# Moving buffers, a transpose and a layer norm in a fused routing attention + MLP kernel

## The chip, the cores and the metric

The kernel runs on one core of one Trainium2 chip, in one launch. The metric is the device time of one execution in microseconds (us): the median of some runs. Engines are TensorE (PE: matmuls, PEld: its weight loads), VectorE (DVE), ScalarE (ACT), GpSimd (POOL, hardly used here) and SyncE (SP, whose queue issues nearly all DMAs). Each engine works off its own instructions in order and waits on semaphores for the others.

## The reference

```
# attention: q, k, v (4, 8, 768, 64), 16 centroids a head
q_assign = argmax(normalize(q) . normalize(centroids)); k_assign likewise
mask   = q_assign == k_assign                 # only same cluster
attn   = softmax(where(mask, q k^T / 8, -1e9))
x      = (attn v) as (4, 768, 512)            # heads side by side
# MLP with a layer norm in front, g_ln its weights
xn     = (x - mean(x)) / sqrt(var(x) + 1e-6) * g_ln
out    = x + relu(xn @ w_ch1) @ w_ch2         # 512 -> 2048 -> 512
```

All inputs but the weights of the MLP are 32-bit floats; w_ch1 and w_ch2 come as 64-bit floats and are turned into 32-bit ones on VectorE, bit by bit, in 32 chunks.

## The kernel before

**Attention.** The work goes over 16 pairs of heads (4 sequences times 4 pairs, numbered 0 to 15). A pair has 12 steps: a step makes the scores of 128 keys against 384 queries for both heads (`scores`, L312: four matmuls into `s_ps`, then ScalarE's exp into a tile `e`) and weighs the values with them (`weigh`, L332, into `a_ps`). VectorE adds each `e` into `es`, the sum for the denominator (L350, L353). Two steps are a slot, six slots (0 to 5) a pair; scores run two steps ahead of the weighing. There are five buffers for `e`, so an exp waits until VectorE has added the `e` of five steps before.

Into the slots other work is put, in a fixed order for TensorE, VectorE and ScalarE (a manual schedule): the next pair's transposes (L230) and cluster assignment (`simT_ps`, L263, in slot 2; VectorE's `best`, `hit`, `first` and the two `onehot` tiles, L270 to L282; their transposes, `oh_ps`, L295, in slot 4), the pair before's denominator (`finish`, L363: `den_ps` in slot 1, in slot 3 the reciprocal and the DMAs that spread it as `rb`, in slot 5 the product `x` and its DMA to memory, `xT_d`), two chunks of weights a pair, and by the table `extra` (`put`, L472) what else is due: the sums of weight blocks `ws` (L166, two in each of pairs 8 to 11) and the layer norm of sequence 0.

**Layer norm of a sequence.** `norm_load` fetches x transposed (`xn`), `norm_rows` transposes 128 rows back (`x_ps`, L412), copies them (`xr`), stores them and takes their statistics (`bn`, `mv`); `norm_stats` makes mean and 1/std of all rows (`stat`, with a square root on ScalarE, L426), transposes them (`stat_ps`, L430) and stores them; `norm_row` fetches them as rows over all partitions; `norm_apply` subtracts (L444) and multiplies (L446), four instructions of VectorE each. `x_sum` (L467) then makes the sums `xt` that the first layer needs.

**MLP.** Per sequence, `first_layer` (L595) makes 16 hidden tiles of 128 x 384 for each half of the rows from seven sums of block products (parts 1 to 7; `x_ps`, `y_ps`, `z_ps`), in which VectorE's `add_relu` (L588) and ScalarE's `kept` (L583) take results out of PSUM. `h0` and `h1` are the tiles of the two halves. Then `project` (L636) makes the six output tiles of the second layer (t = 0 to 5; `o_ps`, 32 matmul instructions each), and between them stands the next sequence's layer norm: its load after t = 0, its rows after t = 1 and t = 2, its statistics, rows and application after t = 2. Only TensorE's order is fixed here; the other engines' order is a scheduler's.

**Memory.** Pools of SBUF lie one behind the other in the order in which they are opened. The pools of attention are closed before the MLP's are opened, and these lie on the same memory: `loads` (12 KB a partition), `heads` (18), `route` (3), `attn` (34.5: `e` first, then `es`, `x`, `dsb`, `rb`) and `conv` (12). The MLP's one pool `ffn` (79 KB) covers them all. `x`, `dsb` and `rb` of pair 15 are the last things that attention uses.

Of the kernel before, what the change touches and what calls it, by code (L numbers as in the profile page):

```python
# [8 lines left out]
F32 = mybir.dt.float32  # L9
# [10 lines left out]
def kernel(  # L20
# [11 lines left out]
    nc = tc.nc  # L32
    B, H, S, D = q.shape
    NCL = centroids.shape[1]
    DM, FF = moe_w_ch1.shape
    P = 128
    NT = S // P
    NHALF = 2
    TH = NT // NHALF
    HC = TH * P  # L40
    Q = 32
    NPAIR = H // 2
    NDC = DM // P
    NFC = FF // P
# [6 lines left out]
    xpool = ctx.enter_context(tc.tile_pool(name="xpool", bufs=1))  # L51
# [4 lines left out]
    def pool(name, bufs, **kw):  # L56
        return stage.enter_context(tc.tile_pool(name=name, bufs=bufs, **kw))

    loads = pool("loads", 1)
    heads = pool("heads", 2)  # L60
    route = pool("route", 1)
    attn = pool("attn", 2)
    conv = pool("conv", 1)
    dram = pool("dram", 4, space=bass.MemoryType.DRAM)
    ps_s = pool("ps_s", 2, space=PSUM)
    ps_a = pool("ps_a", 1, space=PSUM)
# [2 lines left out]
    def ps(name, dt=F32, n=512):  # L69
        return pools["t"].tile([P, n], dt, tag="t", name=name)  # L70
# [24 lines left out]
    ident = const.tile([P, P], F32, name="ident")  # L95
# [211 lines left out]
    xs = {}  # L307
# [24 lines left out]
    def weigh(i):  # L332
        n, g, c = steps[i]
        e = soft[i]
        if c == 0:
            accs[n, g] = ps_a.tile([P, 512], F32, tag="a", name="a_ps")
        acc = accs[n, g]
        for j in range(2):
            nc.tensor.matmul(  # L339
                acc[j * D : (j + 1) * D, :HC],  # L340
                loaded[n]["v"][:, c, j, :],
                e[:, j, :],
                start=(c == 0),
                stop=(c == NT - 1),
            )

        if c == 1:
            es = attn.tile([P, 2, HC], F32, tag="es", name="es", bufs=3)
            sums[n, g] = es
            nc.vector.tensor_tensor(es, soft.pop(i - 1), soft.pop(i), ALU.add)  # L350
        elif c > 1:
            es = sums[n, g]
            nc.vector.tensor_tensor(es, es, soft.pop(i), ALU.add)  # L353
        if c == NT - 1:
            if g == 0:
                xs[n] = attn.tile([P, S], F32, tag="x", name="x", bufs=2)
            nc.scalar.copy(xs[n][:, g * HC : (g + 1) * HC], accs.pop((n, g))[:, :HC])


# [3 lines left out]
    def finish(n, part):  # L363
        b, pr = pairs[n]
        if part == 0:
            den = ps("den_ps")
            for j in range(2):
                for g in range(NHALF):
                    r = (j * NHALF + g) * Q
                    nc.tensor.matmul(  # L370
                        den[r : r + Q, :HC], ones, sums[n, g][:, j, :],
                        start=True, stop=True, tile_position=(0, r),
                    )
            dsb = attn.tile([P, HC], F32, tag="dsb", name="dsb", bufs=1)
            nc.scalar.copy(dsb, den[:, :HC])
            for r in range(0, P, Q):
                nc.sync.dma_start(out=rdens[r : r + Q, n, :], in_=dsb[r : r + 1, :])
        elif part == 1:
            nc.vector.reciprocal(rdens[:, n, :], rdens[:, n, :])
            row = dram.tile([2, S], F32, tag="row", name="row")  # L380
            nc.sync.dma_start(
                out=row.rearrange("j (p e) -> (j p) e", e=DE), in_=rdens[:, n, :]
            )
            rb = attn.tile([P, S], F32, tag="rb", name="rb", bufs=1)
            for j in range(2):
                nc.sync.dma_start(
                    out=rb[j * D : (j + 1) * D, :],
                    in_=row[j : j + 1, :].to_broadcast([D, S]),
                )
            late[n] = rb  # L390
        else:
            x = xs.pop(n)
            nc.vector.tensor_tensor(x, x, late.pop(n), ALU.mult)
            nc.sync.dma_start(out=xT_d[b][pr], in_=x)
# [6 lines left out]
    def norm_load(b):  # L401
        xn = xpool.tile([P, NDC, S], F32, tag="xn", name="xn")
        for c in range(NDC):
            nc.sync.dma_start(out=xn[:, c, :], in_=xT_d[b][c])
        mv = small.tile([P, NT, 2], F32, tag="mv", name="mv")
        normed[b] = [xn, mv]
# [15 lines left out]
    def norm_stats(b):  # L422

        _, mv = normed[b]
        stat = small.tile([P, 2, NT], F32, tag="stat", name="stat")
        nc.scalar.activation(stat[:, 1, :], mv[:, :, 1], AF.Sqrt, bias=eps)  # L426
        nc.vector.tensor_copy(stat[:, 0, :], mv[:, :, 0])
        nc.vector.reciprocal(stat[:, 1, :], stat[:, 1, :])
        sp = ps("stat_ps")
        nc.tensor.transpose(sp[: 2 * NT, :P], stat.rearrange("p s t -> p (s t)"), ident)  # L430
        st = small.tile([2 * NT, P], F32, tag="st", name="st")
        nc.scalar.copy(st, sp[: 2 * NT, :P])
        nc.sync.dma_start(out=stat_d[b].rearrange("s (t p) -> (s t) p", p=P), in_=st)

    def norm_row(b, i):
        row = xpool.tile([P, S], F32, tag="row", name="stat_row", bufs=2)
        nc.sync.dma_start(out=row, in_=stat_d[b][i : i + 1, :].to_broadcast([P, S]))
        normed[b].append(row)

    def norm_apply(b, i, c):  # L440
        xn, row = normed[b][0], normed[b][2 + i]
# [30 lines left out]
    def put(n, slot, f, *args):  # L472
        extra.setdefault((n, slot), []).append(lambda: f(*args))

    put(5, 2, norm_load, 0)
    for t in range(NT):
        put(6 + t, 5, norm_rows, 0, t)
    put(12, 2, norm_stats, 0)
    put(12, 2, norm_row, 0, 0)
    for i in range(2):  # L480
        for c in range(NDC):
            put(13 + i, (2, 3, 4, 5)[c], norm_apply, 0, i, c)
    put(12, 3, norm_row, 0, 1)
    for i in range(4):
        for o in range(2):
            put(8 + 2 * o + i // 2, (0, 3)[i % 2], weight_sum, i, slice(o * WC, (o + 1) * WC))
# [78 lines left out]
    ps_m = pool("ps_m", 2, space=PSUM)  # L565
    pools["t"] = pool("ps_o", 3, space=PSUM)
    ffn = pool("ffn", 2)
    hidden = {}

    def product(bank, lhs, rhs, cols, first):  # L570
# [5 lines left out]
            )  # L576

    def hidden_tile(r, f):
        h = ffn.tile([P, HC], F32, tag=f"h{r}", name=f"h{r}", bufs=NFC + 1)
        hidden[r, f] = h  # L580
        return h

# [43 lines left out]
            add_relu(1, j, st["z"], st["u2"])  # L626

    def rows_load(b, t):
        x = ffn.tile([P, DM], F32, tag="xb", name="xb", bufs=3)
        nc.sync.dma_start(out=x, in_=x_d[b][:, t, :])  # L630
        return x

# [3 lines left out]
    def project(b, t, x, fs, op):  # L636
        r, tt = divmod(t, TH)
        for f in fs:
            nc.tensor.matmul(  # L639
                op,  # L640
                hidden[r, f][:, tt * P : (tt + 1) * P],
                w2[:, f, :],
                start=(f == chunks[0]),
                stop=(f == chunks[-1]),
            )
        if fs[-1] != chunks[-1]:
            return
        o = ffn.tile([P, DM], F32, tag="o", name="o_sb")
        nc.vector.tensor_tensor(o, op, x, ALU.add)  # L649
        nc.sync.dma_start(out=out[b].rearrange("(p c) m -> p c m", p=P)[:, t, :], in_=o)  # L650

    with tc.manual_schedule(engines={mybir.EngineType.PE}):
        for i in range(4):
            x_sum(0, i)
        for b in range(B):
            for j in range(NFH):
                for part, ahead in ((1, 0), (2, 0), (4, 1), (6, 0), (3, 1), (5, 0), (7, 0)):
                    if j - ahead >= 0:
                        first_layer(b, j - ahead, part)
            xb = {0: rows_load(b, 0)}  # L660
            for t in range(NT):
                if t + 1 < NT:
                    xb[t + 1] = rows_load(b, t + 1)
                op = ps("o_ps")
                if t == 0:
                    project(b, t, xb[t], chunks[:-2], op)
                    first_layer(b, NFH - 1, 4)
                    first_layer(b, NFH - 1, 3)
                    project(b, t, xb.pop(t), chunks[-2:], op)
                    if b + 1 < B:  # L670
                        norm_load(b + 1)
                else:
                    project(b, t, xb.pop(t), chunks, op)
                if b + 1 < B:
                    if t in (1, 2):
                        for tt in range(TH):
                            norm_rows(b + 1, (t - 1) * TH + tt)
                    if t == 2:
                        norm_stats(b + 1)
                        for i in range(2):  # L680
                            norm_row(b + 1, i)
                            for c in range(NDC):
                                norm_apply(b + 1, i, c)
                        for i in range(4):
                            x_sum(b + 1, i)

    flag = all_in_range()
    stage.close()
# [198 lines left out]
```

## Time and profile before

| | |
|---|---|
| median of 3 runs | 1072.61 us (1071.07 to 1073.33) |
| the profiled execution | 1072.26 us, its span 1070.5 us |
| TensorE busy | 1020.6 us, 95% of the span |
| VectorE, ScalarE busy | 508.3 us (47%), 314.9 us (29%) |
| chain that ended last | PE 88%, DVE 7%, DMA 2%, issue 1%, ACT 1% |
| mean granted TensorE clock | 0.982 of full speed |

The profile describes one execution. Its page gives busy times, the costliest groups of instructions and the chain of work that ended last; the trace can be asked further, as a timeline (start, duration, engine, line, operation, what it writes and reads, and in brackets how long the engine stood idle before and what released it) or as a list of waits. Attention takes about the first 400 us, the four sequences of the MLP the rest.

### The profile page before, as it was taken

What the parts mean: (1) busy time and instruction counts of PE and PEld (TensorE: products, weight loads), DVE (VectorE), ACT (ScalarE), POOL (GpSimd) and SP (SyncE); (2) the same over time, 40 slices, a digit from 0 to 9 for tenths busy, and PEclk for the clock granted to TensorE, in tenths of its full rate; (3) what the DMA queues carried; (4) which work ended last, traced back from release to release, by engine and by line L of the source; (5) the groups of instructions that cost most, each with busy time, mean ns of one, the idle gap of its engine ahead of it and who ended that gap; (6) DMA issues with size and microseconds to landing.
All of it is one profiled execution on the core that took longest, in us unless ns stands there. A gap on an engine that the chain in (4) does not pass through costs nothing.

```text
span 1070.5 us, 11366 instructions
## 1 busy us (share of the span) xinstructions
PE 1020.6 (95%) x4374; PEld 500.8 (47%) x4374; DVE 508.3 (47%) x860; ACT 314.9 (29%) x516; POOL 2.8 (0%) x27
## 2 busy tenths in 40 slices
PE   6999999999989985999999999989999989999997
PEld 3444444444434432554444555434555434555443
DVE  4888888999998983331141221150221150221000
ACT  4566666666666630220100220000221000221000
POOL 1000000000000000000000000000000000000000
PEclk9999999999999997999999999999999999999999
DMA  7344565545454311002221001231000321000100
GB/s 159 99 135 131 146 168 145 138 129 139 125 139 129 99 66 59 1 0 79 77 71 39 1 1 36 93 98 40 0 1 1 127 80 39 20 0 1 40 29 23
DMA packets 104765, 77.62 MB, mean 73 GB/s; under 512 B 84176, under 2 KB 84224, under 8 KB 104704
## 3 DMA queue, kind: packets, MB, share of 16 engines
q1 hardware_dynamic: 104032, 76.79, 24.9%
q8 instruction: 36, 0.59, 0.2%
q14 instruction: 25, 0.20, 0.1%
q10 hardware_dynamic: 672, 0.03, 0.0%
HBM read 57.71 MB, written 19.00 MB: 72 GB/s over the span
## 4 chain that ended last, share of the span: by engine, by line
PE 88%; DVE 7%; DMA 2%; issue 1%; ACT 1%; SPq 0%; DVEq 0%; ACTq 0%
PE o_ps L639 31%; PE x_ps L572 15%; PE a_ps L339 10%; PE s_ps L324 9%; PE z_ps L572 8%; PE y_ps L572 4%; PE s_ps L319 3%; PE qk_ps L230 2%; DVE es L353 2%; PE sim_ps L247 1%; PE oh_ps L295 1%; PE den_ps L370 1%; PE x_ps L412 1%; DMA x_d<-xr 1%; PE simT_ps L263 1%
## 5 line engine op out<-in xcount | busy, mean ns | idle before, releaser
L639 PE MATMUL o_ps<-w,h 128*128 128x512 f32 x768 | 336.8, 599 | 0.0
L639 PEld LDWEIGHTS o_ps<-w,h 128*128 128x128 f32 x768 | 147.3, 192 | 182.2 <-issue 180.1
L329 ACT ACTIVATE e<-s_ps 128x768 f32<-128x768 f32 x192 | 152.0, 812 | 65.5 <-PE s_ps L324 60.4
L324 PE MATMUL s_ps<-t,t 64*128 64x384 f32 x768 | 157.3, 488 | 0.0
L339 PE MATMUL a_ps<-e,v_sb 128*64 128x384 f32 x768 | 144.8, 499 | 0.0
L590 DVE TENSOR_TENSOR h<-z_ps,u 128x384 f32<-128x384 f32 x64 | 35.7, 557 | 208.7 <-PE z_ps L572 131.7
L353 DVE TENSOR_TENSOR es<-es,e 128x768 f32<-128x768 f32 x128 | 122.2, 955 | 9.5 <-ACT e L329 2.8
L649 DVE TENSOR_TENSOR o_sb<-o_ps,xb 128x512 f32<-128x512 f32 x24 | 16.6, 690 | 212.0 <-PE o_ps L639 212.0
L339 PEld LDWEIGHTS a_ps<-e,v_sb 128*64 128x64 f32 x768 | 46.6, 136 | 86.9 <-issue 85.8
L324 PEld LDWEIGHTS s_ps<-t,t 64*128 64x128 f32 x768 | 69.8, 192 | 22.1 <-issue 22.1
L585 ACT COPY u<-x_ps 128x384 f32<-128x384 f32 x64 | 30.6, 478 | 139.7 <-PE x_ps L572 139.7
L585 ACT COPY p<-x_ps 128x384 f32<-128x384 f32 x32 | 15.3, 478 | 167.6 <-PE x_ps L572 154.3
L319 PE MATMUL s_ps<-m,m 64*128 64x384 bf16 x384 | 64.3, 331 | 0.0
L572 PE MATMUL x_ps<-xt,ws 128*128 128x384 f32 x128 | 48.0, 498 | 12.6 <-DMA xb<-x_d 12.6
L572 PE MATMUL z_ps<-xt,ws 128*128 128x384 f32 x128 | 47.8, 497 | 0.0
L623 ACT ACTIVATE h<-x_ps 128x384 f32<-128x384 f32 x32 | 15.7, 490 | 108.8 <-PE x_ps L572 108.8
L572 PE MATMUL x_ps<-xn,w 128*128 128x384 f32 x128 | 47.4, 493 | 0.0
L572 PE MATMUL x_ps<-xn,ws 128*128 128x384 f32 x128 | 46.8, 488 | 0.0
L572 PE MATMUL y_ps<-xn,w 128*128 128x384 f32 x128 | 46.5, 486 | 0.0
L572 PE MATMUL x_ps<-xt,w 128*128 128x384 f32 x128 | 46.5, 486 | 0.0
L572 PE MATMUL z_ps<-xn,ws 128*128 128x384 f32 x128 | 46.5, 486 | 0.0
L416 ACT COPY xr<-x_ps 128x512 f32<-128x512 f32 x24 | 13.5, 587 | 98.0 <-PE x_ps L412 82.8
(101 smaller groups left out, 797.9 us busy)
## 6 DMA issues: line engine op xcount, KB each, us to landing
raw<-in_moe_w_ch_dram SPq DMA_DIRECT2D x32, 512.0 KB, 3.8
q_sb<-in_q_dram SPq DMA_DIRECT2D x32, 192.0 KB, 4.4
k_sb<-in_k_dram SPq DMA_DIRECT2D x32, 192.0 KB, 4.4
v_sb<-in_v_dram SPq DMA_DIRECT2D x32, 192.0 KB, 4.1
rb<-row SPq DMA_DIRECT2D x32, 192.0 KB, 3.3
xT_d<-x SPq DMA_DIRECT2D x16, 384.0 KB, 2.9
xn<-xT_d SPq DMA_DIRECT2D x16, 384.0 KB, 4.5
x_d<-xr SPq DMA_DIRECT2D x24, 256.0 KB, 2.8
```

The source lines that it names most:

```text
L230: nc.tensor.transpose(t[:, c * P : (c + 1) * P], src[:, g * TH + c, :, :].rearrange("p h d -> p (h d)"), ident,)
L319: nc.tensor.matmul(s[:, j, :HC], st["m", 1][rows[j], keys], st["m", 0][rows[j], cols], start=True, stop=False,)
L324: nc.tensor.matmul(s[:, j, :HC], st[1][rows[j], keys], st[0][rows[j], cols], start=False, stop=True,)
L329: nc.scalar.activation(e, s[:, :, :HC], AF.Exp, scale=SCALE)
L339: nc.tensor.matmul(acc[j * D : (j + 1) * D, :HC], loaded[n]["v"][:, c, j, :], e[:, j, :], start=(c == 0), stop=(c == NT - 1),)
L353: nc.vector.tensor_tensor(es, es, soft.pop(i), ALU.add)
L572: nc.tensor.matmul(bank[:, :HC], lhs[:, c, cols], rhs[:, c, :], start=first and c == 0, stop=c == NDH - 1, skip_group_check=True,)
L585: nc.scalar.copy(t, bank[:, :HC])
L590: nc.vector.tensor_tensor(h, bank[:, :HC], other, ALU.add)
L623: nc.scalar.activation(hidden_tile(0, NFH + j), st["x"][:, :HC], AF.Relu)
L639: nc.tensor.matmul(op, hidden[r, f][:, tt * P : (tt + 1) * P], w2[:, f, :], start=(f == chunks[0]), stop=(f == chunks[-1]),)
L649: nc.vector.tensor_tensor(o, op, x, ALU.add)
```

## The change

Three things are changed.

The pools: `conv` is opened before `attn`; `es`, `x`, `dsb` and `rb` get a pool of their own, `last`, opened behind them all. The MLP's pool is cut in two: `ffn` now ends where `conv` ends, give or take 1.7 KB, and so lies on `loads`, `heads`, `route` and `conv`; the second, `ffn1` (`h1`, `xb`, `o_sb`), lies on the end of `conv`, on `attn` and `last`. `h1` is first written by part 7 of the first layer (VectorE's h<-z_ps).

The statistics: making `stat` and transposing it are now two functions, `norm_stats` and `norm_stat_rows`. In the MLP the transpose stands in the middle of t = 3, and the application follows t = 4.

The norm of sequence 0: its load moves from slot 2 to slot 1 of pair 5, its six groups of rows from slot 5 of pairs 6 to 11 to slots 3 and 5 of pairs 5 to 8, the statistics from slot 2 of pair 12 to slot 0 of pair 9 (the transpose to its slot 3), and the eight instructions of `norm_apply` from slots 2 to 5 of pairs 13 and 14 to slots 2 and 5 of pairs 10 to 13.

```diff
     route = pool("route", 1)
+    conv = pool("conv", 1)
     attn = pool("attn", 2)
-    conv = pool("conv", 1)
+    last = pool("last", 1)
...
-            es = attn.tile([P, 2, HC], F32, tag="es", name="es", bufs=3)
+            es = last.tile([P, 2, HC], F32, tag="es", name="es", bufs=3)
... (x, dsb and rb likewise)
         nc.vector.reciprocal(stat[:, 1, :], stat[:, 1, :])
+        normed[b][1] = stat
+
+    def norm_stat_rows(b):
         sp = ps("stat_ps")
-        nc.tensor.transpose(sp[: 2 * NT, :P], stat.rearrange("p s t -> p (s t)"), ident)
+        nc.tensor.transpose(
+            sp[: 2 * NT, :P], normed[b][1].rearrange("p s t -> p (s t)"), ident
+        )
         st = small.tile([2 * NT, P], F32, tag="st", name="st")
         nc.scalar.copy(st, sp[: 2 * NT, :P])
         nc.sync.dma_start(out=stat_d[b].rearrange("s (t p) -> (s t) p", p=P), in_=st)
-
-    def norm_row(b, i):
-        row = xpool.tile([P, S], F32, tag="row", name="stat_row", bufs=2)
-        nc.sync.dma_start(out=row, in_=stat_d[b][i : i + 1, :].to_broadcast([P, S]))
-        normed[b].append(row)
+        for i in range(2):
+            row = xpool.tile([P, S], F32, tag="row", name="stat_row", bufs=2)
+            nc.sync.dma_start(out=row, in_=stat_d[b][i : i + 1, :].to_broadcast([P, S]))
+            normed[b].append(row)
...
-        put(6 + t, 5, norm_rows, 0, t)
+        put(5 + (t + 1) // 2, (3, 5)[(t + 1) % 2], norm_rows, 0, t)
...
-            put(13 + i, (2, 3, 4, 5)[c], norm_apply, 0, i, c)
+            put(10 + 2 * i + c // 2, (2, 5)[c % 2], norm_apply, 0, i, c)
...
     ffn = pool("ffn", 2)
+    ffn1 = pool("ffn1", 1)
...
-        h = ffn.tile([P, HC], F32, tag=f"h{r}", name=f"h{r}", bufs=NFC + 1)
+        h = (ffn, ffn1)[r].tile([P, HC], F32, tag=f"h{r}", name=f"h{r}", bufs=NFC + 1)
... (xb and o_sb go to ffn1)
                 op = ps("o_ps")
+                cut = -2 if t == 0 else NFC // 2
+                project(b, t, xb[t], chunks[:cut], op)
                 if t == 0:
...
+                if t == 3 and b + 1 < B:
+                    norm_stat_rows(b + 1)
+                project(b, t, xb.pop(t), chunks[cut:], op)
...
                     if t == 2:
                         norm_stats(b + 1)
-                        for i in range(2):
-                            norm_row(b + 1, i)
-                            for c in range(NDC):
-                                norm_apply(b + 1, i, c)
-                        for i in range(4):
-                            x_sum(b + 1, i)
+                elif t == 4:
+                    for i in range(2):
+                        for c in range(NDC):
+                            norm_apply(b + 1, i, c)
+                    for i in range(4):
+                        x_sum(b + 1, i)
```

**In the second layer,** TensorE's instructions around the end of t = 2 (`x_ps` are the rows of the next sequence, `stat_ps` the statistics, `o_ps` the output tiles) stood so before:

```order
L639 MATMUL o_ps<-w_161,h_5352 128x512
L412 MATMUL x_ps<-ident,xn 128x128 x12
L430 MATMUL stat_ps<-ident,stat 12x128
L639 MATMUL o_ps<-w_161,h_5114 128x512
L639 MATMUL o_ps<-w_161,h_5090 128x512
```

Now they stand so:

```order
L413 MATMUL x_ps<-ident,xn 128x128 x12
L644 MATMUL o_ps<-w_164,h_5121 128x512
L644 MATMUL o_ps<-w_164,h_5097 128x512
L644 MATMUL o_ps<-w_164,h_5155 128x512
L644 MATMUL o_ps<-w_164,h_5131 128x512
L644 MATMUL o_ps<-w_164,h_5189 128x512
L644 MATMUL o_ps<-w_164,h_5165 128x512
L644 MATMUL o_ps<-w_164,h_5223 128x512
L644 MATMUL o_ps<-w_164,h_5199 128x512
L434 MATMUL stat_ps<-ident,stat 12x128
L644 MATMUL o_ps<-w_164,h_5257 128x512
```

The statistics' transpose has moved behind eight of the sixteen pairs of matmuls of t = 3.

**Where attention ends,** VectorE's instructions after the last sums `es` (`ends` is a test of the denominators, `xt` and the `xn` between them are `x_sum`, `h` the hidden tiles, `x` the last product with `rb`) stood so before:

```order
L554 TENSOR_TENSOR ends<-ends 128x1
L393 TENSOR_TENSOR x<-x,rb 128x768
L467 TENSOR_TENSOR xt_4053<-xn 128x768
L590 TENSOR_TENSOR h_4068<-y_ps,p_4063 128x384
L467 TENSOR_TENSOR xt_4054<-xn,xt_4053 128x768
L467 TENSOR_TENSOR xn<-xn 128x2x384
L467 TENSOR_TENSOR xt_4055<-xn,xt_4054 128x768
```

Now they stand so:

```order
L472 TENSOR_TENSOR xt_4060<-xn 128x768
L472 TENSOR_TENSOR xt_4061<-xn,xt_4060 128x768
L472 TENSOR_TENSOR xn<-xn 128x2x384
L472 TENSOR_TENSOR xt_4062<-xn,xt_4061 128x768
L595 TENSOR_TENSOR h_4075<-y_ps,p_4070 128x384
L596 TENSOR_SCALAR h_4075<-h_4075 128x384
L380 RECIPROCAL rdens<-rdens 128x12
...
L558 TENSOR_TENSOR ends<-ends 128x1
L595 TENSOR_TENSOR h_4100<-y_ps,p_4095 128x384
L596 TENSOR_SCALAR h_4100<-h_4100 128x384
L394 TENSOR_TENSOR x<-x,rb 128x768
L595 TENSOR_TENSOR h_4089<-z_ps,u_4087 128x384
```

The four instructions of `x_sum` and two hidden tiles from `y_ps` have moved ahead of the product with `rb`; the first tile from `z_ps`, which is the first one of `ffn1`, stands behind it.

**In attention,** VectorE's instructions in slots 2 and 3 of pair 10 stood so before:

```order
L282 TENSOR_TENSOR onehot_k<-rev,first 128x12x16
L353 TENSOR_TENSOR es<-es,e 128x768 x2
L350 TENSOR_TENSOR es<-e 128x768
L379 RECIPROCAL rdens<-rdens 128x12
L196 TENSOR_SCALAR ta<-raw 128x512
```

Now they stand so:

```order
L283 TENSOR_TENSOR onehot_k<-rev,first 128x12x16
L354 TENSOR_TENSOR es<-es,e 128x768 x2
L449 TENSOR_TENSOR xn<-xn,stat_row 128x768
L351 TENSOR_TENSOR es<-e 128x768
L380 RECIPROCAL rdens<-rdens 128x12
```

A subtraction of the norm now stands between the sums `es`, beside the weight sums that this pair has as before; pairs 10 and 11 have two such subtractions each, pairs 12 and 13 two multiplications.

## Rows read from the trace of the kernel before

**Rows 1.** TensorE's waits: waiting line <- waited for: total us, times, longest.
```profile
PE stat_ps L430 <- DVE stat L428: 17.2, 4, 5.0
PE x_ps L572 <- DMA xb<-x_d: 12.6, 1, 12.6
...
PE den_ps L370 <- DVE es L353: 4.1, 2, 3.6
```

**Rows 2.** Timeline, second layer of sequence 0: start, us, engine, line, operation, [idle before].
```profile
517.63 13.90 PE L639 MATMUL o_ps<-w,h 128*128 128x512 f32 x32
...
531.37 1.60 PE L412 MATMUL x_ps<-ident,xn 128*128 128x128 f32 x12
...
537.39 0.19 DVE L428 RECIPROCAL stat<-stat 128x6 f32<-128x6 f32 x1 [0.49 <-ACT stat L426]
...
537.64 0.28 PE L430 MATMUL stat_ps<-ident,stat 128*12 128x128 f32 x1 [4.66 <-DVE stat L428]
...
537.75 22.46 PE L639 MATMUL o_ps<-w,h 128*128 128x512 f32 x48
...
543.24 3.56 DVE L444 TENSOR_TENSOR xn<-xn,stat_row 128x768 f32<-128x768 f32 x4 [5.66 <-DMA stat_row<-stat_d]
```

**Rows 3.** Timeline of TensorE, pairs 11 to 15.
```profile
285.59 0.55 PE L263 MATMUL simT_ps<-ident,sim_sb 128*128 128x128 f32 x3
...
293.99 0.33 PE L319 MATMUL s_ps<-m,m 64*128 64x384 bf16 x2
...
309.29 0.55 PE L263 MATMUL simT_ps<-ident,sim_sb 128*128 128x128 f32 x3
...
316.26 0.38 PE L430 MATMUL stat_ps<-ident,stat 128*12 128x128 f32 x1 [3.27 <-DVE stat L428]
...
337.64 0.55 PE L263 MATMUL simT_ps<-ident,sim_sb 128*128 128x128 f32 x3
...
360.91 0.55 PE L263 MATMUL simT_ps<-ident,sim_sb 128*128 128x128 f32 x3
...
379.33 0.85 PE L370 MATMUL den_ps<-es,ones 128*32 128x384 f32 x6 [0.52 <-DVE es L353]
```

**Rows 4.** Timeline of VectorE, pairs 5, 11 and 13.
```profile
144.41 0.56 DVE L270 TENSOR_REDUCE best<-simT_ps 128x24 f32<-128x384 f32 x1 [1.93 <-PE simT_ps L263]
...
288.06 0.55 DVE L270 TENSOR_REDUCE best<-simT_ps 128x24 f32<-128x384 f32 x1
...
295.24 1.22 DVE L166 TENSOR_TENSOR ws<-w,ws 128x1024 f32<-128x1024 f32 x1
...
343.06 0.95 DVE L444 TENSOR_TENSOR xn<-xn,stat_row 128x768 f32<-128x768 f32 x1
```

**Rows 5.** Timeline of ScalarE, pairs 11 and 12.
```profile
292.01 0.81 ACT L329 ACTIVATE e<-s_ps 128x768 f32<-128x768 f32 x1 [0.93 <-DVE es L353]
...
313.54 1.28 ACT L426 ACT_TABLE_LOAD   x1
314.84 0.30 ACT L426 ACTIVATE stat<-mv,eps 128x6 f32<-128x6 f32 x1
```

**Rows 6.** Timeline, end of attention and start of the MLP.
```profile
398.48 1.50 PE L370 MATMUL den_ps<-es,ones 128*32 128x384 f32 x6 [3.61 <-DVE es L353]
...
404.31 0.23 DVE L379 RECIPROCAL rdens<-rdens 128x12 f32<-128x12 f32 x1 [5.02 <-DMA rdens<-dsb]
...
410.30 0.96 DVE L393 TENSOR_TENSOR x<-x,rb 128x768 f32<-128x768 f32 x1 [4.73 <-DMA rb<-row]
...
413.71 0.96 DVE L467 TENSOR_TENSOR xt<-xn 128x768 f32<-128x768 f32 x1 [2.45 <-DMA xT_d<-x]
...
416.10 2.90 PE L572 MATMUL x_ps<-xt,ws 128*128 128x384 f32 x4 [12.59 <-DMA xb<-x_d]
...
428.10 1.45 PE L572 MATMUL z_ps<-xn,ws 128*128 128x384 f32 x4
```

**Rows 7.** Stretch from the last pair into the MLP: busy us of engines, PEclk.
```profile
394.00:434.00 40.00, 23.80 (x65) 12.50 (x64) 15.20 (x28) 4.79 (x10) 0.00 (x0) 0.79 0.17 59
```

More of the change, by code (lines that the diff above doesn't have):

```diff
@@ L355, in weigh @@
             if g == 0:
-                xs[n] = attn.tile([P, S], F32, tag="x", name="x", bufs=2)
+                xs[n] = last.tile([P, S], F32, tag="x", name="x", bufs=2)
             nc.scalar.copy(xs[n][:, g * HC : (g + 1) * HC], accs.pop((n, g))[:, :HC])
@@ L373, in finish @@
                     )
-            dsb = attn.tile([P, HC], F32, tag="dsb", name="dsb", bufs=1)
+            dsb = last.tile([P, HC], F32, tag="dsb", name="dsb")
             nc.scalar.copy(dsb, den[:, :HC])
@@ L383, in finish @@
             )
-            rb = attn.tile([P, S], F32, tag="rb", name="rb", bufs=1)
+            rb = last.tile([P, S], F32, tag="rb", name="rb")
             for j in range(2):
@@ L473, in put @@
         extra.setdefault((n, slot), []).append(lambda: f(*args))
-    put(5, 2, norm_load, 0)
+    put(5, 1, norm_load, 0)
     for t in range(NT):
-        put(6 + t, 5, norm_rows, 0, t)
-    put(12, 2, norm_stats, 0)
-    put(12, 2, norm_row, 0, 0)
+        put(5 + (t + 1) // 2, (3, 5)[(t + 1) % 2], norm_rows, 0, t)
+    put(9, 0, norm_stats, 0)
+    put(9, 3, norm_stat_rows, 0)
     for i in range(2):
         for c in range(NDC):
-            put(13 + i, (2, 3, 4, 5)[c], norm_apply, 0, i, c)
-    put(12, 3, norm_row, 0, 1)
+            put(10 + 2 * i + c // 2, (2, 5)[c % 2], norm_apply, 0, i, c)
     for i in range(4):
@@ L628, in rows_load @@
     def rows_load(b, t):
-        x = ffn.tile([P, DM], F32, tag="xb", name="xb", bufs=3)
+        x = ffn1.tile([P, DM], F32, tag="xb", name="xb", bufs=3)
         nc.sync.dma_start(out=x, in_=x_d[b][:, t, :])
@@ L647, in project @@
             return
-        o = ffn.tile([P, DM], F32, tag="o", name="o_sb")
+        o = ffn1.tile([P, DM], F32, tag="o", name="o_sb", bufs=2)
         nc.vector.tensor_tensor(o, op, x, ALU.add)
@@ L664 @@
                 op = ps("o_ps")
+                cut = -2 if t == 0 else NFC // 2
+                project(b, t, xb[t], chunks[:cut], op)
                 if t == 0:
-                    project(b, t, xb[t], chunks[:-2], op)
                     first_layer(b, NFH - 1, 4)
                     first_layer(b, NFH - 1, 3)
[L669 to L677, printed above, removed]
+                if t == 3 and b + 1 < B:
+                    norm_stat_rows(b + 1)
+                project(b, t, xb.pop(t), chunks[cut:], op)
+                if b + 1 == B:
+                    continue
+                if t == 0:
+                    norm_load(b + 1)
+                elif t < 3:
+                    for tt in range(TH):
+                        norm_rows(b + 1, (t - 1) * TH + tt)
                     if t == 2:
                         norm_stats(b + 1)
-                        for i in range(2):
-                            norm_row(b + 1, i)
-                            for c in range(NDC):
-                                norm_apply(b + 1, i, c)
-                        for i in range(4):
-                            x_sum(b + 1, i)
+                elif t == 4:
[4 more added lines that the diff above has]
+                        x_sum(b + 1, i)
     flag = all_in_range()
```

## Prediction

> **What bounds the kernel now.** I read the busy times first: TensorE works 1020.6 of 1070.5 us, so only what makes it stand still, or slows it, can be won. The list of its waits comes next [rows 1]: apart from the start it has three large entries. Four times it waits for `stat` before the statistics' transpose (17.2 us), once at the start of the MLP (12.6 us), and twice for the sums `es` before a denominator (4.1 us). These are the places that the change touches. The timeline then shows what each of them costs beyond the wait, for after a long one TensorE goes on at half speed: six `den_ps` matmuls took 0.85 us after a wait of 0.52 us [rows 3] and 1.50 us after one of 3.61 us [rows 6], and the stretch from the last pair into the MLP has a granted clock of 0.79 [rows 7], a mixture of the two levels, 2.4 and 1.2 GHz.
>
> **Statistics in the MLP, three times.** After t = 2 TensorE ends its transposes at 532.97 (531.37 + 1.60), waits 4.66 us for `stat` and takes up the second layer at 537.75 [rows 2]. The next 48 matmuls take 22.46 us; at the rate of the 32 at full speed (13.90 / 32 = 0.434 us) they would take 20.85. So one such place costs 4.66 us of waiting and 1.6 us of slow clock. The transpose itself stays, 0.1 us before the next matmul starts. In the new place it comes eight of sixteen parts later, some 6.9 us after t = 3 begins at about 533, thus near 539.8; `stat` is ready at 537.58 (537.39 + 0.19), so it finds its data with 2 us to spare. The page's 17.2 us, less the 3.27 us of pair 12 [rows 3], leave 13.9 us for three places; with 3 x 1.6 us of clock that is **18.7 us**. What is late next? VectorE's norm starts 5.6 us after the transpose (543.24 - 537.64) and has 12 instructions of about 0.95 us [rows 2, 4]: from 545.4 it is done near 557. The next sequence starts when t = 3 to 5 have run, 3 x 13.9 us after 533, at 574. That is hidden with 17 us left.
>
> **Pair 12.** From one `simT_ps` to the next, pair 12 to 13 takes 28.35 us (337.64 - 309.29), the plain one after it 23.27 (360.91 - 337.64) [rows 3]. The 5.1 us between are the wait of 3.27 us, the transpose and a slow clock behind it. In pair 9 three slots lie between making `stat` and transposing it, so nothing waits; the transpose keeps at most 0.3 us: **4.8 us** gained. The moved rows cost TensorE what they did (a pair with them has 23.70 us, 309.29 - 285.59, against 23.27), and their load has four slots to land. On SP's queue the statistics' store and fetches now stand in pair 9, ahead of a load of q that is used six slots later.
>
> **What pair 9 gets for it: two table loads.** ScalarE's square root needs its table loaded and exp's loaded again, now with slot 1's copies between. The row shows 1.28 us for one, and the root starting at once behind it, at 314.84 [rows 5]. Two and the root are 2.9 us, spread over slots 0 to 2 of an engine that is busy 29% of the span; I count nothing, with 2.9 us as the other end. The Trainium skill, "ScalarE: Activation LUTs", section "What ACT_TABLE_LOAD costs", adds a drain of some 1.38 us to every load. By it the two loads would be 2.8 us dearer and the sum up to as much worse; the row, with no gap behind the load, speaks against it here.
>
> **VectorE in pairs 8 to 13.** This is the part that costs. In a pair without extras VectorE idles 1.93 us before `best` [rows 4], so it needs 21.3 of 23.27 us. A weight sum is 1.22 us and a subtraction 0.95 [rows 4], less about 0.1 us each by which the next starts early. Before, pairs 8 to 11 (two weight sums and one group of rows) already outran it: in pair 11 `best` starts 1.92 us after its `simT_ps` has ended (288.06 against 286.14 [rows 3, 4]), from nothing in pair 7, so about 0.5 us of debt a pair. By pair 10 the debt is about 1.4 us, before as after. From there the subtractions take the place of the rows: per pair +1.7 us for the two, -0.8 for the rows' statistics, and TensorE's pair is 0.43 us shorter, so the debt grows by 0.5 + 1.3 = 1.8 us in pair 10 and by 0.7 in pair 11 (one weight sum less to the next `best`), to about 4 us. How much does TensorE stand? In pair 11 the second exp of slot 3 waited 0.93 us for a sum `es` and ended at 292.82 [rows 5]; TensorE needs its PSUM buffer at 293.99 [rows 3], 1.1 us later. So about 3 us of debt are free, and what is beyond stops TensorE: **1.2 us lost**, bounds 0 and 4 (if all the debt were paid). Waits this short left the clock high at 379.33 [rows 3].
>
> **End of attention.** Before, VectorE entered pair 13 without debt (the stop in pair 12 let it catch up), and took eight norm instructions there and in pair 14: 7.6 us. Now it enters with up to 3 us and takes two, 1.9 us. That is 2.7 us less debt at the last denominators, whose waits are 4.1 us [rows 1]: I take **2.6 us** gained, bounds 0 and 4.1.
>
> **Start of the MLP.** Before, `p1`, `xt` and all else of `ffn` wait for the DMA that stores the last `x`: VectorE's `xt` at 413.71, TensorE's part 6 at 416.10 [rows 6]. That wait covers the whole pool, and `ffn` no longer lies on `x` and `rb`. So `x_sum` runs right behind the sums, done about 4.5 us after 398.48, and TensorE goes on through parts 6, 5, 7 and the next tile's 1, 2, 4, 6: seven products of 1.29 us (four matmuls each) from about 403.5, to 412.5. Then comes part 3 of tile 0, which accumulates into `z_ps`, and it must wait until VectorE has taken h out of that bank. This h is the first tile of `ffn1`, which does lie on `x`. So VectorE stands there until the store has landed: at 413.65 before, and now some 0.45 us later, for the second `y_ps` tile, ready near 410, stands ahead of the product that began at 410.30 [rows 6]. Part 3 then starts near 414.75 (414.1, the addition 0.55, a semaphore) in place of 428.10 [rows 6]: 13.4 us. TensorE has stood 2.3 us there; for the slow clock behind it I take off 1.5 us, as in pair 12 (5.1 less 3.27 and the transpose): **11.9 us** gained. Bounds: 15.6 if part 3 needs not wait (412.5), 0 if everything stands until the store as before.
>
> **The sum.** 18.7 + 4.8 - 1.2 + 2.6 + 11.9 = 36.8 us. From the profiled execution, 1072.26 us (span 1070.5), that gives 1035.5; its time is 0.35 us below the median of the runs shown, which is less than anything here is known to. I predict **1035.5 us**.
>
> **Rivals.** (1) *The wait at the start of the MLP only moves.* The pools are cut, but `ffn1` still lies on the last buffers, and a stopped VectorE, with all that is queued behind its h<-z_ps, could hold up as much as before. For it: VectorE is in order, and the first tile of `ffn1` comes early. Against: nine products of TensorE stand ahead of the first that needs it. Then the 11.9 us go: 1047.4. (2) *VectorE's debt costs several times more.* Pairs 8 to 11 are its tightest, and each stop also delays exps. If all of the debt of 4 us is paid and the last denominators gain nothing, 2.8 + 2.6 us go: 1040.9. (3) *ScalarE has no room in pair 9.* If the two loads and the root (2 x 1.28 + 0.30 us [rows 5]) delay the exps by all they take, TensorE stands 2.9 us: 1038.4. For it: each exp is waited for two steps later, and VectorE's sums come late besides; against: in slot 1 TensorE has `sim_ps` and `den_ps` to do meanwhile (six matmuls of the latter are 0.85 us [rows 3]). The drain that the Trainium skill's "ScalarE: Activation LUTs" adds would bring this about; the row at 314.84 does not bear it out. (4) *Slower than before.* TensorE's clock falls in attention. It fell after waits of 3.27 and 3.61 us, not after 0.52; nothing here shows what many waits of about a microsecond do. If those in pairs 10 to 13 brought it to 1.2 GHz, a pair of 23.27 us of TensorE work would take twice that. The change turns into a loss when the low level lasts 36.8 / 23.27 = 1.6 pairs; two pairs give 1035.5 + 46.5 = 1082. Against: the estimate has one or two stops of under a microsecond, and TensorE is 95% busy around them.
>
> **Chances.** The forecast, with its small terms within their bounds, 0.76, and its own range 1031 to 1040; rival 1 0.12, rival 2 0.07, rival 3 0.03, rival 4 0.02. The range, 1030 to 1044, leaves out rival 1 at its full size, rival 4, and the best ends all together (1072.26 - 18.7 - 4.8 - 4.1 - 15.6 = 1029). Differences under 0.2% (2 us) cannot be told from no change here. All cases but rival 4 are faster by far more: faster 0.97, the same 0.01, slower 0.02.
>
> **What the profile after would show.** TensorE's list of waits should have no entry for `stat_ps` over 0.5 us; the clock should be full through t = 3 and 4; pair 12 should be as long as pair 14 to within 1 us; the delay of `best` behind `simT_ps` should rise to about 3 us by pairs 11 and 12, with small waits of TensorE for `oh_ps` or the exps there. After the last denominator TensorE should run into tile 1's products and wait two or three us once, at `z_ps`, for VectorE's h, and that for the last store. The prediction is wrong if this wait is near 10 us, if TensorE stops in pairs 10 to 12 for more than 4 us, or if a new wait stands at the start of sequences 1 to 3.

## The result, and the profile after

The changed kernel takes **1035.35 us** (median of 4 runs, 1034.77 to 1035.58), the kernel before 1072.16 (median of 4, 1071.07 to 1073.33): a ratio of 0.9656, with a 95% interval of 0.9639 to 0.9672. The forecast was 1035.5. The profiled execution took 1035.45 us, its span is 1033.6.

First TensorE's waits, as in [rows 1] (line, tile, releaser: us in total, times, the longest one):

```profile
PE ct_ps L143 <- DVE c_sb L138: 4.8, 1, 4.8
PE oh_ps L296 <- DVE onehot_q L283: 3.0, 2, 2.8
PE den_ps L371 <- DVE es L354: 2.4, 1, 2.4
PE z_ps L577 <- DVE h L595: 2.4, 1, 2.4
```

The first entry and 2.8 us of the second belong to the start-up. `stat_ps` (17.2 us before) is gone, `den_ps` has fallen from 4.1 to 2.4, and for the 12.6 us at `x_ps` there now stand 2.4 at `z_ps`. The stretches from 500 to 1020 us (busy us of PE, PEld, DVE, ACT and POOL, granted clock, DMA share, GB/s) show the MLP. First before:

```profile
500.00:1020.00 520.00, 506.09 (x1389) 258.88 (x1388) 128.35 (x244) 59.24 (x122) 0.00 (x0) 0.99 0.13 43
```

and after:

```profile
500.00:1020.00 520.00, 520.00 (x1426) 264.89 (x1425) 127.54 (x243) 58.13 (x119) 0.00 (x0) 1.00 0.12 41
```

TensorE stood 13.9 us there and now stands for nothing. The timeline answers to [rows 2], in the same MLP of sequence 0 (start, us, engine, line, operation, [idle before]):

```profile
513.30 1.60 PE L413 MATMUL x_ps<-ident,xn 128*128 128x128 f32 x12
514.74 7.03 PE L644 MATMUL o_ps<-w,h 128*128 128x512 f32 x16
...
519.30 0.19 DVE L429 RECIPROCAL stat<-stat 128x6 f32<-128x6 f32 x1 [0.50 <-ACT stat L427]
...
521.61 0.27 PE L434 MATMUL stat_ps<-ident,stat 128*12 128x128 f32 x1
521.72 23.77 PE L644 MATMUL o_ps<-w,h 128*128 128x512 f32 x55
...
537.91 0.95 DVE L472 TENSOR_TENSOR xt<-xn,xt 128x768 f32<-128x768 f32 x1
```

The reciprocal is ready at 519.49, the transpose comes at 521.61: 2.1 us to spare. The 55 matmuls behind it take 23.77 / 55 = 0.432 us each, full speed. VectorE's norm ends at 538.86.

TensorE in pairs 11 to 14, which answers to [rows 3]:

```profile
287.19 0.55 PE L264 MATMUL simT_ps<-ident,sim_sb 128*128 128x128 f32 x3
...
296.05 0.34 PE L320 MATMUL s_ps<-m,m 64*128 64x384 bf16 x2 [0.28 <-ACT e L330]
...
310.93 0.55 PE L264 MATMUL simT_ps<-ident,sim_sb 128*128 128x128 f32 x3
...
318.02 0.51 PE L296 MATMUL oh_ps<-identb,onehot_q 128*128 128x128 bf16 x6 [0.23 <-DVE onehot_q L283]
...
320.06 0.34 PE L320 MATMUL s_ps<-m,m 64*128 64x384 bf16 x2 [0.28 <-ACT e L330]
...
334.94 0.55 PE L264 MATMUL simT_ps<-ident,sim_sb 128*128 128x128 f32 x3
...
358.20 0.55 PE L264 MATMUL simT_ps<-ident,sim_sb 128*128 128x128 f32 x3
```

and VectorE's `best` in pairs 11, 12 and 13 ([rows 4]):

```profile
291.24 0.55 DVE L271 TENSOR_REDUCE best<-simT_ps 128x24 f32<-128x384 f32 x1
...
315.25 0.55 DVE L271 TENSOR_REDUCE best<-simT_ps 128x24 f32<-128x384 f32 x1
...
338.25 0.55 DVE L271 TENSOR_REDUCE best<-simT_ps 128x24 f32<-128x384 f32 x1
```

Pair 11 to 12 takes 23.74 us, 12 to 13 takes 24.01, 13 to 14 the plain 23.26. So 0.48 + 0.75 = 1.2 us are lost: 0.8 in three stops of 0.2 to 0.3 us, the rest beside them. `best` starts 3.5, 3.8 and 2.8 us after its `simT_ps` has ended.

Last, the start of the MLP, which answers to [rows 6]:

```profile
393.21 0.85 PE L371 MATMUL den_ps<-es,ones 128*32 128x384 f32 x6 [2.39 <-DVE es L354]
...
393.98 1.56 PE L577 MATMUL x_ps<-xn,w 128*128 128x384 f32 x4
...
403.39 0.56 DVE L595 TENSOR_TENSOR h<-y_ps,p 128x384 f32<-128x384 f32 x1 [3.75 <-PE y_ps L577]
...
404.26 0.95 DVE L394 TENSOR_TENSOR x<-x,rb 128x768 f32<-128x768 f32 x1
...
407.62 0.56 DVE L595 TENSOR_TENSOR h<-z_ps,u 128x384 f32<-128x384 f32 x1 [2.41 <-DMA xT_d<-x]
...
408.23 1.70 PE L577 MATMUL z_ps<-xn,ws 128*128 128x384 f32 x4 [2.37 <-DVE h L595]
...
409.73 2.76 PE L577 MATMUL z_ps<-xt,ws 128*128 128x384 f32 x4
...
412.29 1.77 PE L577 MATMUL x_ps<-xn,ws 128*128 128x384 f32 x4
...
413.90 1.45 PE L577 MATMUL x_ps<-xn,w 128*128 128x384 f32 x4
```

TensorE runs through tile 0's parts and into tile 1's, until part 3 of tile 0 (408.23). It needs a bank from which VectorE takes h, that h is the first tile of `ffn1`, and it waits for the store of the last `x`. The matmul at 413.90 is part 1 of tile 2. The stretch of [rows 7] has a granted clock of 0.96 instead of 0.79.

### The profile page after: what moved, and what is told of

It reads as the page before. It is cut to its first block, busy times and chain, and to the rows that moved or that the text cites. A ratio compares the mean times of both kernels' runs of the same rounds, so it can differ in the third digit from the quotient of the medians.

```text
span 1033.6 us, 11347 instructions
## 1 busy us (share of the span) xinstructions
PE 1011.8 (98%) x4374; PEld 498.2 (48%) x4374; DVE 508.2 (49%) x860; ACT 314.9 (30%) x516; POOL 2.8 (0%) x27
## 4 chain that ended last, share of the span: by engine, by line
PE 88%; DVE 9%; issue 1%; DMA 1%; ACT 0%; SPq 0%; DVEq 0%; ACTq 0%
PE o_ps L644 32%; PE x_ps L577 16%; PE a_ps L340 9%; PE s_ps L325 9%; PE z_ps L577 8%; PE y_ps L577 4%; PE s_ps L320 3%; DVE es L354 3%; PE qk_ps L231 2%; PE x_ps L413 1%; PE sim_ps L248 1%; PE oh_ps L296 1%; PE den_ps L371 1%; DVE es L351 1%; DVE ws L167 1%
## 5 line engine op out<-in xcount | busy, mean ns | idle before, releaser
L644 PE MATMUL o_ps<-w,h 128*128 128x512 f32 x768 | 332.2, 592 | 0.0
L644 PEld LDWEIGHTS o_ps<-w,h 128*128 128x128 f32 x768 | 145.2, 190 | 178.7 <-issue 176.6
```

Of the source, the lines that this page charges most:

```text
L644: nc.tensor.matmul(op, hidden[r, f][:, tt * P : (tt + 1) * P], w2[:, f, :], start=(f == chunks[0]), stop=(f == chunks[-1]),)
```

## Experiments

Theory A is the working of the prediction: three parts that add up, and at the start of the MLP a wait that follows the pools' bounds and VectorE's order. The rivals name themselves in the expectations. The first four kernels ran beside one set of runs of the kernel before (median 1073.19 of 7), the last four beside another (1072.58 of 9).

**e1_mlp_stats: only the statistics in the MLP**

```diff
-                    project(b, t, xb.pop(t), chunks[-2:], op)
...
+                if t == 3 and b + 1 < B:
+                    norm_stat_rows(b + 1)
+                project(b, t, xb.pop(t), chunks[cut:], op)
```

> Before, with one part of the change: in the MLP the statistics' transpose in mid t = 3 and the norm applied after t = 4. Pools and the norm of sequence 0 as before. My theory (each stop costs its wait and the slow clock behind it): the three waits of 13.9 us and 3 x 1.6 us of half-speed matmuls go, 18.7 us: 1072.2 - 18.7 = 1053.5 us, and the only wait left for stat_ps is the one of 3.3 us in pair 12. Rival A (the slow matmuls behind the stops are not due to them): only the 13.9 us of waiting go, 1058.3 us. Rival B (the norm, moved to t = 4, holds up the next sequence): less than 13.9 us, with a new wait of TensorE for xn or xt at the start of sequences 1 to 3.

Measured: 1053.42 us (1051.37 to 1054.14), ratio 0.9818 (0.9799 to 0.9838), or -19.8 us. Of the waits for `stat` one of 3.3 us is left, pair 12's; `x_ps` (11.6) and `den_ps` (4.2) stay. The term of 18.7 us holds by itself: rival A's 1058.3 us lies above all four runs, and rival B's wait for `xn` or `xt` is not in the list.

**e2_pools: only the pools**

```diff
+    last = pool("last", 1)
...
-                xs[n] = attn.tile([P, S], F32, tag="x", name="x", bufs=2)
+                xs[n] = last.tile([P, S], F32, tag="x", name="x", bufs=2)
...
-        h = ffn.tile([P, HC], F32, tag=f"h{r}", name=f"h{r}", bufs=NFC + 1)
+        h = (ffn, ffn1)[r].tile([P, HC], F32, tag=f"h{r}", name=f"h{r}", bufs=NFC + 1)
```

> Before, with one part of the change: the pools (conv ahead of attn, es, x, dsb and rb in a pool of their own at the end, the MLP's pool cut in two). My theory: TensorE runs on behind the last denominators until it needs the z_ps bank whose h waits for the last store; 11.9 us, for VectorE is as late there as before: about 1060.3 us, with one wait of 2 to 3 us at z_ps in place of the 12.6 us. The 3.6 us before den_ps stay. Rival (the wait only moves): 1070 to 1072 us, a wait near 10 us or more at z_ps or at the first products.

Measured: 1063.01 us (1062.50 to 1064.89), ratio 0.9916 (0.9897 to 0.9935), or -10.2 us, 2.7 above the figure expected. TensorE's timeline from the last denominators, without the rows between:

```profile
399.37 1.50 PE L371 MATMUL den_ps<-es,ones 128*32 128x384 f32 x6 [3.63 <-DVE es L354]
...
415.82 2.80 PE L574 MATMUL z_ps<-xn,ws 128*128 128x384 f32 x4 [2.40 <-DVE h L592]
...
421.49 1.45 PE L574 MATMUL x_ps<-xn,w 128*128 128x384 f32 x4
```

From the denominators to part 1 of tile 2 it is 22.12 us, 33.49 before (431.97 - 398.48): 11.4 us of the 11.9 are there, with the wait for h in the place and size foreseen. Another 1.4 us were lost in the profiled MLP: from the first to the second `stat_ps` it is 165.17 us here and 163.79 before, though the waits for it add up to the same (17.1 and 17.2 us). Those places, each with a slow clock behind it, scatter by that much: from the second to the third it is 163.80 us here and 164.44 before. Another 0.7 us stand in the start-up (28.24 us to pair 0's `simT_ps`, 27.51 before).

**e3_norm0: only the first sequence's norm**

```diff
-    put(12, 2, norm_stats, 0)
-    put(12, 2, norm_row, 0, 0)
+    put(9, 0, norm_stats, 0)
+    put(9, 3, norm_stat_rows, 0)
...
-            put(13 + i, (2, 3, 4, 5)[c], norm_apply, 0, i, c)
+            put(10 + 2 * i + c // 2, (2, 5)[c % 2], norm_apply, 0, i, c)
```

> Before, with one part of the change: the norm of sequence 0 in pairs 5 to 13 (with the statistics' transpose three slots behind the statistics). Pools and MLP as before. My theory: pair 12's stop goes (5.1 us less 0.3), TensorE stands about 1.2 us in pairs 11 and 12 for VectorE, and the denominators at the end wait 1.5 us instead of 4.1, 2.6 us less with the slow clock behind them gone: 6.2 us together, 1066.0 us; the wait at the start of the MLP is still 12 to 13 us. Rival A (the debt costs nothing, and the end gains by itself): 7.4 us or more, 1064.8. Rival B (the gain at the end is the pools', not this part's): 3.6 us, 1068.6, the wait before den_ps still about 3.6 us.

Measured: 1066.16 us (1064.23 to 1066.49), ratio 0.9935 (0.9917 to 0.9953), or -7.0 us; `den_ps` is down to one wait of 2.4 us, not to the 1.5 expected, and `best` is late by 3.5, 3.8, 2.8 and 2.5 us in pairs 11 to 14, as in the whole change. By time alone rival A (7.4 us) is not told apart from the theory; the trace does it, for pairs 11 and 12 take 23.77 and 24.02 us against 23.26, so the debt costs 1.3 us. The three parts alone give -19.8, -10.2 and -7.0, together -37.0; the whole gave -36.8. They add.

**e4_h1_ffn: the second h in the first pool**

```diff
-        h = (ffn, ffn1)[r].tile([P, HC], F32, tag=f"h{r}", name=f"h{r}", bufs=NFC + 1)
+        h = ffn.tile([P, HC], F32, tag=f"h{r}", name=f"h{r}", bufs=NFC + 1)
```

> The changed kernel with h1 in the MLP's first pool, so that this pool ends 0.2 KB a partition short of where x of the last pair begins; it covers es, which lies in the same pool as x, dsb and rb. Theory A (a new pool waits for every pool that it touches as a whole): all of the first pool waits for the last store again, and the start of the MLP loses its gain of 12.8 us: 1035.4 + 12.8 = 1048.2 us, with a wait of 12 to 13 us at the first product that reads xt. Theory B (the wait goes by the bytes of the single buffers): nothing of the MLP's first tiles waits for the store, and the wait of 2.4 us at z_ps and the slow matmuls behind it go: about 1031.5 us.

Measured: 1047.20 us (1046.08 to 1048.06), ratio 0.9766 (0.9748 to 0.9784). The wait is back whole in the list of TensorE's waits:

```profile
PE x_ps L577 <- DMA xb<-x_d: 11.9, 1, 11.9
```

and in VectorE's timeline the first sum `xt` stands for the store of `x`, as before the change:

```profile
407.52 0.96 DVE L472 TENSOR_TENSOR xt<-xn 128x768 f32<-128x768 f32 x1 [2.45 <-DMA xT_d<-x]
```

By the sizes in the kernel, `ffn` now ends 0.2 KB below `x`, but reaches into the pool `last`, by way of `es`. No byte of it lies on what the store reads, and all of it waits for the store: the wait follows pools, not bytes. That is theory A's reading, and its figure was 1048.2. It is also close to the price of the prediction's rival 1 (1047.4), but by another way: here the first pool waits, while rival 1 had TensorE held up behind VectorE's h from `z_ps`.

**e5_after_again: the changed kernel as a yardstick**

> The changed kernel once more, beside the next three, as their yardstick: 1035.4 us, waits of 2.4 us before den_ps and 2.4 us at z_ps, and some 1.2 us that pairs 11 and 12 are longer than a plain one.

Measured: 1035.13 us (1034.70 to 1036.09), ratio 0.9651 (0.9637 to 0.9664). It is the same kernel profiled a second time, and both waits and what follows them come out as in the first profile:

```profile
393.04 0.85 PE L371 MATMUL den_ps<-es,ones 128*32 128x384 f32 x6 [2.37 <-DVE es L354]
393.81 1.56 PE L577 MATMUL x_ps<-xn,w 128*128 128x384 f32 x4
...
408.19 1.77 PE L577 MATMUL z_ps<-xn,ws 128*128 128x384 f32 x4 [2.50 <-DVE h L595]
409.76 2.77 PE L577 MATMUL z_ps<-xt,ws 128*128 128x384 f32 x4
```

Pairs 11 and 12 take 23.77 and 24.00 us.

**e7_es_pool: as e4, and `es` out of the pool `last`**

```diff
+    sums_pool = pool("sums", 1)
     last = pool("last", 1)
...
-            es = last.tile([P, 2, HC], F32, tag="es", name="es", bufs=3)
+            es = sums_pool.tile([P, 2, HC], F32, tag="es", name="es", bufs=3)
```

> The changed kernel with h1 in the MLP's first pool and es in a pool of its own between attn and last, so that the first pool touches no pool in which x, dsb or rb lie. Theory (the 2.4 us at z_ps are the price of h1 lying on the last pair's buffers): this wait goes and with it the slow matmuls behind it, 2.4 + 1.5 us less: about 1031.5 us; the 2.4 us before den_ps stay. Rival (VectorE is in order and stands for rb before it takes z_ps, whatever h1 lies on): no gain, 1035 us or more, with a wait at z_ps that ends when the last product is done.

Measured: 1030.38 us (1029.95 to 1032.04), ratio 0.9607 (0.9594 to 0.9620); 4.75 below the changed kernel. TensorE's timeline:

```profile
392.46 0.85 PE L372 MATMUL den_ps<-es,ones 128*32 128x384 f32 x6 [2.37 <-DVE es L355]
393.23 2.38 PE L578 MATMUL x_ps<-xn,w 128*128 128x384 f32 x4
395.40 2.37 PE L578 MATMUL y_ps<-xn,w 128*128 128x384 f32 x4
397.61 1.45 PE L578 MATMUL x_ps<-xt,ws 128*128 128x384 f32 x4
...
406.64 1.45 PE L578 MATMUL z_ps<-xn,ws 128*128 128x384 f32 x4
```

Part 3 (406.64) waits for nothing: with h in a pool that touches none of the last `x`, the wait at `z_ps` is gone, as the theory says. The rival was not put to the test in its own terms, for the scheduler now sets VectorE's first h from `z_ps` (402.19) ahead of the product with `rb` (405.20); that the store alone held h up is read in the changed kernel, where the product was done at 405.21 and h stood until 407.62 for `xT_d`. In the program the only difference between e4 and e7 is the pool in which `es` lies (by the sizes in the kernel it lies at the same bytes in both): 16.8 us, the two having run beside different sets of the kernel before.

**e8_weights_early: three of the weight chunks earlier**

```diff
+    done = [0]
+    MORE = {(1, 5), (3, 5), (5, 2)}
+    LEFT = {(11, 3), (13, 3), (15, 3)}
...
+            if slot % 3 == 0 and (n, slot) not in LEFT:
+                split_weight(done[0])
...
+            elif (n, slot) in MORE:
+                split_weight(done[0])
+                join_weight(done[0])
```

> The changed kernel with three of the 32 weight chunks turned on VectorE earlier: one more in each of pairs 1, 3 and 5, where it idles 1.9 us a pair, and one less in pairs 11, 13 and 15. No work is left out. Theory (what TensorE loses in pairs 11 and 12 and before the last denominators is VectorE's debt): the 1.2 us go, and of the 2.4 us before den_ps at least 2, so 3.2 us less: about 1032.2 us, with VectorE at most 2 us behind in pairs 11 to 14. Rival (the 2.4 us are the way from the last exp over the sum to TensorE, whatever VectorE did before): only the 1.2 us go, 1034.2 us, and the wait before den_ps stays at 2 us or more.

Measured: 1029.99 us (1028.53 to 1030.65), ratio 0.9600 (0.9587 to 0.9613); 5.1 below the changed kernel, 2.2 more than expected. TensorE's timeline:

```profile
388.87 0.85 PE L371 MATMUL den_ps<-es,ones 128*32 128x384 f32 x8
...
403.90 1.56 PE L585 MATMUL z_ps<-xn,ws 128*128 128x384 f32 x4 [2.38 <-DVE h L603]
405.30 1.45 PE L585 MATMUL z_ps<-xt,ws 128*128 128x384 f32 x4
```

The eight denominators run in one piece, so VectorE's lateness was what they waited for, and the rival is refuted. Now VectorE waits for ScalarE's last exps:

```profile
386.29 2.02 DVE L354 TENSOR_TENSOR es<-es,e 128x768 f32<-128x768 f32 x2 [1.14 <-ACT e L330]
```

But the edit takes away two things at once. VectorE's debt is gone by pair 14 (`best` is late by 3.5, 0.7, 0.4 and 0.0 us in pairs 11 to 14, where the changed kernel has 2.5 in pair 14), and so is the chunk of pair 15, some 3.9 us of VectorE's work right in front of the last sums. By these rows either could have ended the wait by itself (an estimate: 2.5 us of debt or a chunk of 3.9 against a wait of 2.4); which of them did was not tried. What is left of the debt costs one pair 0.46 us (310.55 less 286.83 between its `simT_ps`, against 23.26). The two us more: the stop at the denominators cost 3.2 us rather than the 2.4 of its wait (from the first of them to the first product it was 393.98 - 389.99 = 3.99 us and is 389.65 - 388.87 = 0.78), where 2 had been counted, and the wait at `z_ps`, as long as before, is not followed by a slow clock (1.7 us less).

**e9_both: e7 and e8 together**

> The two edits before together (es in its own pool with h1 in the first one, and three weight chunks earlier). If the two costs are apart: 3.9 + 3.2 us less, about 1028.3 us, and TensorE has no wait of over 1 us between the first pair and the end. Rival (without the wait for the last denominators TensorE only comes to z_ps earlier, and VectorE's product with rb holds it up there): no better than the better one of the two, about 1031.5 us.

Measured: **1025.86 us** (1025.70 to 1026.15), ratio 0.9563 (0.9550 to 0.9576), the fastest here, 9.3 below the changed kernel; e7 and e8 alone give 4.75 + 5.1. It is also 2.4 below the 1028.3 expected, which added the two sizes foreseen (3.9 + 3.2) and not the two measured. The wait at `z_ps` is gone here too, so the rival is refuted. After the start-up TensorE's longest wait is 0.6 us:

```profile
PE ct_ps L144 <- DVE c_sb L139: 4.8, 1, 4.8
PE oh_ps L297 <- DVE onehot_q L284: 2.8, 1, 2.8
PE simT_ps L265 <- ACT sim_sb L258: 0.6, 1, 0.6
```

## Why the prediction was right

The difference of the two spans, 1070.5 - 1033.6 = 36.9 us, can be cut at four of TensorE's instructions and laid beside the sum of 36.8.

- **Statistics in the MLP, 18.7 us.** From part 1 of tile 2 (431.97 before, 413.90 after) to the end it is 638.53 and 619.70 us: **18.8**. e1 has 19.8 for it by medians.
- **Pair 12 and VectorE's debt, 4.8 - 1.2 = 3.6 us.** From pair 0's `simT_ps` (27.51 and 28.44) to pair 14's (360.91 and 358.20) it is 333.40 and 329.76: **3.6**. The loss of 1.2 us is read apart, in the two long pairs above. Rival 2, several times that, is refuted; the debt grew to 3.8 us, "about 4".
- **End of attention, 2.6 us.** From there to the last six denominators, 37.57 and 35.01: **2.6**. The size is right partly by luck. The waits fell by 1.7 us (4.1 to 2.4), for the last one shrank to 2.4 us and not to the 1.5 that the working implies. The rest is what a stop costs beside its wait, which the working had at nothing: from the two `den_ps` to the next scores it was 380.10 - 377.97 = 2.13 us in pair 15 before, with a wait of 0.52, and is 376.05 - 375.26 = 0.79 without one, so that short stop had cost 1.3 us.
- **Start of the MLP, 11.9 us.** From the denominators to part 1 of tile 2, 33.49 and 20.69: **12.8**, within its bounds of 0 and 15.6. What was off was the clock at the denominators: behind a wait of 2.39 us they and the first product ran at full speed (0.85 us against 1.50, 1.56 against 2.31), where I had counted no gain. TensorE itself gains nothing by that, since it stands at `z_ps` later; but the way to the store gets shorter. VectorE's product with `rb` begins 11.05 us behind the denominators (404.26 - 393.21) and not the 12.3 of my working: the reciprocal comes 0.6 us earlier (5.19 us behind them, 5.83 before), and the product 5.9 us behind it (6.0 before), so that the second `y_ps` tile, there earlier, does not set it back. Behind the wait at `z_ps` the slow clock cost 1.8 us (5.67 from 408.23 to 413.90 against three products of 1.29) where I had taken 1.5. That TensorE waits 2.37 us there and VectorE stands with h for the store came as worked out, so rival 1, a wait near ten us, is refuted; e4 and e7 show that the pools' bounds decide it, both ways.
- **The table loads, 0 us.** ScalarE's timeline in pair 9:

```profile
235.48 1.28 ACT L427 ACT_TABLE_LOAD   x1
236.77 0.30 ACT L427 ACTIVATE stat<-mv,eps 128x6 f32<-128x6 f32 x1
236.98 0.46 ACT L257 COPY sim_sb<-sim_ps 128x384 f32<-128x384 f32 x1
237.54 0.48 ACT L376 COPY dsb<-den_ps 128x384 f32<-128x384 f32 x1
238.03 1.28 ACT L330 ACT_TABLE_LOAD   x1
239.33 1.51 ACT L330 ACTIVATE e<-s_ps 128x768 f32<-128x768 f32 x2
```

Both loads take 1.28 us, with the next instruction 0.01 and 0.02 us behind them, and TensorE has no wait there, so rival 3 is refuted. The drain of some 1.38 us that the Trainium skill, "ScalarE: Activation LUTs", section "What ACT_TABLE_LOAD costs", adds does not show here, on a busy engine either.

- **Rival 4.** Waits of 0.2 to 0.3 us in pairs 11 and 12 left the clock high: the plain pair after them has its 23.26 us.

The remaining -0.9 us is the start-up, 27.51 and 28.44 us before pair 0's `simT_ps`, which the change doesn't touch; the same kernel had 28.28 in e5, and e7 and e9 have 27.72 and 27.81. So the sum is not right by luck of large errors that cancel: each term is within 1 us of its own stretch. That it is right to 0.1 us is luck, for the largest misses, 0.9 gained at the start of the MLP and 0.9 lost in the start-up, cancel.

## What to carry to other kernels

Where a new pool takes over space, ask which whole pools it touches and what the last user of each of them waits for: 16.8 us hung on which pool a buffer of sums was in. Work that makes an engine late is paid only beyond the slack that its consumers have (of 3.8 us of debt 1.2 were paid). What is left of it can be collected at the next place where that engine is waited for at once, here perhaps the last denominators (e8 does not part the debt from the chunk that stood there); work that has no date is best moved to pairs with idle time, and away from such a place (e8). A stop can cost more than its wait: 0.8 us more at the denominators, where two matmuls take 0.83 us and eight 0.85, so that two runs take nearly twice as long as one, and sometimes a slow clock behind it.

## What was not expected of the hardware

Waits of nearly one length were followed by different clocks. The 2.39 us at `den_ps` in the changed kernel left the next products at full speed (1.56 us for four matmuls), 2.37 us at the same place in e7 were followed by two slow products (2.38, 2.37; granted clock 0.61 from 393.2 to 397.6, a mixture of the two levels), and so were 2.41 us there in e4 (2.40, 2.35). 2.37 us at `z_ps` were followed by slow products (2.76 for four, granted clock 0.70 from 408.2 to 413.9) in the changed kernel, 2.38 us in e8 by none (1.56, 1.45, granted clock 1.00). Even behind 3.62 us at `den_ps` in e1 the six denominators took 0.85 us, and the products behind them were the slow ones (2.88, 1.87). So the length of the wait alone does not tell whether 1.8 us are lost behind it, nor how soon the slow clock begins, and e7's and e8's single profiles carry that much of chance. The one kernel that was profiled twice, the changed one (e5), fell the same way both times at both places; two profiles are too few to say that a kernel always does, and what decides it stays open.
